# A 64-byte touch of every sixteenth QKV weight row, issued from ScalarE's queue ahead of the weight loads

## The chip, the cores and the metric

One core of a Trainium2 chip. The metric is device time in microseconds (us) of one execution; lower is better. Each execution also has a span, the time from its first to its last instruction, which is on record to 0.1 us. PE's granted clock is the share of its full clock that it was given, a mean over the execution. Engines: PE is TensorE (PEld its weight loads), DVE VectorE, ACT ScalarE, POOL GpSimd, SP SyncE; a "q" behind a name is its DMA-issuing queue.

## The reference, cut to what matters

```python
def reference(A_x, A_wqkv, A_wo, B_x, B_w_gate, B_w_up, B_w_down):
    x = A_x                                   # 1 x 2048 x 640, bf16
    xn = layernorm(x)
    # A: q, k, v = xn @ A_wqkv (640 x 1920); 32 heads of 20; each position attends
    #    to 8 earlier ones, 2 apart; then @ A_wo
    # B: ((xn @ w_gate) * (xn @ w_up)) @ w_down, 640 -> 1536 -> 640
    return x + A(xn) + B(xn)
```

Everything waits for the layer norm and for the first matmuls with `A_wqkv`, so the kernel begins with loads of x tiles (128 rows each) and of the QKV weights in chunks of 128 rows. The Q part, the K part and the V part of one weight row stand side by side in memory.

## The kernel before

The kernel records its operations with what each reads and writes, and derives the waits from that. The opening loads, in the order of issue:

```python
    op("act", ... ACT.Sqrt ..., name="sqrt_preload")
    for half, eng in ((0, "sp"), (1, "act")):          # x tile 0, half from each queue
        dst = XST[:, 0, half * DHALF:(half + 1) * DHALF]
        dma(dst, xhbm[0:TS, half * DHALF:(half + 1) * DHALF], w=[dst], name=f"xh{half}", eng=eng)
    x_load(1)                                          # all that follows is issued by SP
    for c in range(NCH):                               # NCH = 5
        wqkv_load(0, c)                                # Q weights, 160 KB a chunk
    x_load(2)
    x_load(3)
    for c in range(NCH):
        wqkv_load(1, c)                                # K weights
    ...
```

And the start of PE's work. Tile 0's Q projection goes through the chunks in order; of the five transposes of x tile 1, two stand between chunk 3 and chunk 4 and three within chunk 4:

```python
    bm = 1
    proj_tile(0, [(0, 0)], bm, {(4, 0): lambda: ln_pe(1, 0, 2), (4, 3): lambda: tr(1, 2)})
    part_evac(0, 0, 1, 0, 4, 0, 0)
    proj_tile(0, [(1, 2)], bm)
    ...
```

Of the kernel before, what the change touches and what calls it, by code (L numbers as in the profile page):

```python
# [10 lines left out]
D = 640  # L11
# [30 lines left out]
class Sched:  # L42
# [20 lines left out]
    def keys(self, x):  # L63
# [10 lines left out]
        for step, n in reversed(dims[1:]):  # L74
# [4 lines left out]
            else:  # L79
                starts = [s + i * step for s in starts for i in range(n)]  # L80
        if name == "PS":
            spans = {(s * es // 2048, (s + run - 1) * es // 2048) for s in starts}
# [130 lines left out]
def build_kernel(nc, A_x, A_wqkv, A_wo, B_x, B_w_gate, B_w_up, B_w_down, out):  # L213
# [5 lines left out]
    def sb(name, shape, dtype=BF16, at=None):  # L219
        n = mybir.dt.size(dtype)  # L220
        for s in shape[1:]:
            n *= s
        n = (n + 63) // 64 * 64
        if at is None:
            at = place[0]
            place[0] += n
        assert at + n <= 229344, (name, at + n)
        return K.sbuf(name, shape, dtype, at)
# [9 lines left out]
    a_pv = place[0]  # L238
# [46 lines left out]
    IDENT = sb("IDENT", [128, 128])  # L285
    MASK = sb("MASK", [128, W, PAD], FP16)
    MSK0 = sb("MSK0", [128, W, PAD], FP16)
    PS = nc.alloc_psum_tensor("PS", [128, 8, 512], FP32)
    xhbm = A_x[0]
    ohbm = out[0]  # L290

    def dma(o, i, r=(), w=(), name="", eng="sp", group=None):
        return op(eng, lambda e: e.dma_start(o, i), r=r, w=w, dma=True, name=name, group=group)
# [10 lines left out]
    op("dve", lambda e: e.memset(MASK[:], 0.0), w=[MASK[:]], name="mask0")  # L304
    op("dve", lambda e: e.memset(MSK0[:], 0.0), w=[MSK0[:]], name="msk0")
    op("pool", lambda e: e.affine_select(MSK0[:], MSK0[:], pattern=[[DIL, W], [1, PAD]], compare_op=ALU.is_ge, fill=NEG,
                                         base=-PAD, channel_multiplier=0), r=[MSK0[:]], w=[MSK0[:]], name="msk1")

    def x_load(t, eng="sp"):
        dma(XST[:, t % NXS, :], xhbm[t * TS:(t + 1) * TS, :], w=[XST[:, t % NXS, :]], name=f"xld{t}", eng=eng)  # L310
# [7 lines left out]
    def wqkv_load(g, c=None, eng="sp"):  # L318
        cs = slice(0, NCH) if c is None else c
        dst = WQKV[:, g, cs]  # L320
        dma(dst, wqkv_src[:, cs, g * D:(g + 1) * D], w=[dst], name=f"ld_wqkv{g}_{c}", eng=eng)

    op("act", lambda e: e.activation(DUM[:, 0:1], EPSC[:, 0:1], ACT.Sqrt), r=[EPSC[:]], w=[DUM[:]], name="sqrt_preload")
    for half, eng in ((0, "sp"), (1, "act")):
        dst = XST[:, 0, half * DHALF:(half + 1) * DHALF]
        dma(dst, xhbm[0:TS, half * DHALF:(half + 1) * DHALF], w=[dst], name=f"xh{half}", eng=eng)
    x_load(1)
    for c in range(NCH):
        wqkv_load(0, c)
# [12 lines left out]
    def late_loads():  # L342
        dma(MASK[0:128:4], MSK0[0:32], r=[MSK0[0:32]], w=[MASK[0:128:4]], name="mask")
        wqkv_load(2)
        for T, src in ((WG, B_w_gate), (WU, B_w_up)):
            dma(T[:], src.rearrange("(c p) n -> p c n", p=128), w=[T[:]], name="ld_w")
# [10 lines left out]
    def tp_view(t, c0, c1):  # L357
# [3 lines left out]
        if t == 1 and c0 > 1:  # L361
            b = 4
        return PS[:, b, :].bitcast(BF16)[:, c0 * 128:c1 * 128].rearrange("p (c f) -> p c f", c=c1 - c0)

# [82 lines left out]
    def warm(n, wide=JB):  # L447
        z = ZERO[:, 0:1].to_broadcast([128, wide])
        for _ in range(n):
            op("pe", lambda e: e.matmul(PS[:, 5, 0:wide], ZERO[:], z, start=True, stop=True), r=[ZERO[:]], w=[PS[:, 5, :]],  # L450
               name="warm")
# [9 lines left out]
    def wcols(which, c, m):  # L461
        return WQKV[:, which, c, m:D:NCH]
# [5 lines left out]
    def proj(which, m, j):  # L468
        b = bank()
        for c in range(NCH):  # L470
            l, x = wcols(which, c, m), XNT[:, c, j * JB:(j + 1) * JB]
            op("pe", (lambda l, x, c: lambda e: e.matmul(PS[:, b, :], l, x, start=(c == 0), stop=(c == NCH - 1)))(l, x, c),  # L472
               r=[l, x], w=[PS[:, b, :]], name=f"p{which}_{m}_{j}_{c}")
        if which == 2:
            o = VO[:, m, VP + j * JB:VP + (j + 1) * JB]
        else:
            o = qk_dst(which, m, j * JB, JB)
        sc = SCALE if which == 0 else 1.0
        op("act", lambda e: e.activation(o, PS[:, b, :], ACT.Copy, scale=sc), r=[PS[:, b, :]], w=[o],
           name=f"pev{which}_{m}_{j}")  # L480
# [463 lines left out]
def bass_parallel_sum__sliding_local_dilated__glu_gated_bilinear__prompt_kernel(  # L944
    nc, A_x, A_wqkv, A_wo, B_x, B_w_gate, B_w_up, B_w_down, out
):
    build_kernel(nc, A_x, A_wqkv, A_wo, B_x, B_w_gate, B_w_up, B_w_down, out)
# [28 lines left out]
```

## Time and profile before

| | |
|---|---|
| time, median of the first 3 runs | 254.32 us (254.29 to 254.47) |
| span of the profiled run | 252.4 us |
| PE busy | 98% |
| PE's share of the chain that ended last | 96% |
| start of PE's unbroken run | 7.84 us |

How to read it: PE is the bound nearly everywhere. What isn't PE lies in the first 8 us, where x tiles and weights come in and the first layer norms run. The chain of waits before begins PE's first group without further stops, 57 matmuls, at 7.84 and ends with the last addition on DVE:

```profile
7.84 3.32 PE PS L500 x57
...
250.20 0.22 DVE FOUT L691
```

(Columns: start, duration in us, engine and what.) From the first of these to the second are 242.36 us. If the start moves and the distance stays, the end moves with the start.

### The profile page before, as it was taken

The numbers are of one execution on the slowest core, as the hardware profiler recorded it, in microseconds if no ns is written. First come the engines' busy times: TensorE is split into PE (matmuls) and PEld (weight loads), VectorE is DVE, ScalarE is ACT, GpSimd is POOL, SyncE is SP. The second block draws the span as 40 slices with busy tenths as digits, with TensorE's granted clock in tenths as the row PEclk, the third lists the DMA queues.
The fourth block names the chain that finished last, engine by engine and source line by source line (L and its number), as shares of the span: only waits on it lengthen the run. The fifth ranks groups of instructions, "written<-read, shape, count | busy, mean of one in ns | idle before, by whom it ended". The sixth has DMA issues, their size and how long they took to land.

```text
span 252.4 us, 3908 instructions
## 1 busy us (share of the span) xinstructions
PE 248.1 (98%) x1607; PEld 149.2 (59%) x1622; DVE 215.1 (85%) x254; ACT 113.9 (45%) x202; POOL 35.9 (14%) x44
## 2 busy tenths in 40 slices
PE   8999999999999999999999999999999999999996
PEld 3999855555544444444444457764444777777775
DVE  4899799999999954999999974899999999995221
ACT  5486675555555557555555552225555112112000
POOL 1000001044425331003411100101000010111000
DMA  6988789956777562536379931393000021330511
GB/s 201 297 177 164 117 205 395 277 109 114 134 137 128 92 125 44 199 134 124 57 138 314 429 101 23 37 347 55 0 0 0 3 32 20 55 45 9 104 52 52
DMA packets 25664, 31.83 MB, mean 126 GB/s; under 512 B 9744, under 2 KB 22160, under 8 KB 25616
## 3 DMA queue, kind: packets, MB, share of 16 engines
q1 hardware_dynamic: 19120, 22.15, 28.9%
q0 software_dynamic: 6240, 9.31, 23.0%
q8 instruction: 12, 0.20, 0.3%
q10 hardware_dynamic: 288, 0.15, 0.2%
q14 instruction: 4, 0.03, 0.0%
HBM read 14.42 MB, written 4.59 MB: 75 GB/s over the span
## 4 chain that ended last, share of the span: by engine, by line
PE 96%; ACT 1%; DMA 1%; DVE 1%; issue 0%
PE PS L646 41%; PE PS L677 29%; PE PS L472 17%; PE PS L487 4%; PE PS L507 2%; PE PS L500 2%; DMA XST<-in_A_x_dram 1%; ACT XNS L391 0%; PE PS L431 0%; ACT XNS L389 0%; DVE STATS L369 0%; DVE STATS L375 0%; DVE XNS L416 0%; ACT SD L394 0%; ACT SD L382 0%
## 5 line engine op out<-in xcount | busy, mean ns | idle before, releaser
L646 PE MATMUL PS<-XNT,WU 128*128 128x512 bf16 x240 | 59.6, 379 | 0.0
L646 PE MATMUL PS<-XNT,WG 128*128 128x512 bf16 x229 | 57.3, 379 | 0.6
L613 DVE TENSOR_TENSOR PVB<-VO,ATB 128x10240 f16<-128x10240 bf16 x8 | 43.9, 5492 | 0.1
L677 PE MATMUL PS<-WD,HT 128*128 128x320 bf16 (+2 forms) x300 | 43.2, 294 | 0.0
L472 PE MATMUL PS<-XNT,WQKV 128*128 128x512 bf16 x196 | 43.0, 379 | 0.2
L646 PEld LDWEIGHTS PS<-XNT,WU 128*128 128x128 bf16 x240 | 23.5, 98 | 28.3
L646 PEld LDWEIGHTS PS<-XNT,WG 128*128 128x128 bf16 x240 | 23.5, 98 | 28.1
L648 ACT ACTIVATE USX<-PS 128x512 bf16<-128x512 f32 x48 | 28.7, 597 | 22.2 <-PE PS L646 21.7
L677 PEld LDWEIGHTS PS<-WD,HT 128*128 128x128 bf16 x300 | 28.7, 98 | 11.0
L472 PEld LDWEIGHTS PS<-XNT,WQKV 128*128 128x128 bf16 x200 | 23.5, 118 | 19.5
L608 DVE TENSOR_TENSOR PVB<-PVB 128x5120 f16<-128x5120 f16 (+1 forms) x16 | 34.6, 2160 | 0.3
L541 POOL DMA_DIRECT2D LOG<-PE x24 | 21.9, 939 | 60.9 <-DMA LOG<-PE 60.9
L648 ACT ACTIVATE HT<-PS 128x512 bf16<-128x512 f32 x36 | 21.5, 597 | 16.8 <-PE PS L646 16.8
L686 ACT ACTIVATE FACC<-PS 128x640 f16<-128x640 f32 x12 | 8.4, 703 | 44.1 <-PE PS L677 44.1
L677 PE MATMUL PS<-WO,VO 128*128 128x320 bf16 (+2 forms) x165 | 27.1, 295 | 0.0
L677 PEld LDWEIGHTS PS<-WO,VO 128*128 128x128 bf16 x165 | 15.9, 98 | 5.9
L530 DVE TENSOR_TENSOR PP<-QH,KH 128x2048 f16<-128x2048 bf16 x16 | 19.1, 1221 | 0.0
L530 DVE TENSOR_TENSOR TMP<-QH,KH 128x2048 f16<-128x2048 bf16 x16 | 19.0, 1221 | 0.0
L535 DVE TENSOR_TENSOR PP<-PP,TMP 128x4096 f16<-128x4096 f16 x8 | 18.3, 2292 | 0.2
L701 POOL DMA_DIRECT2D out_dram<-FACC x6 | 7.1, 1186 | 74.7 <-ACT FACC L686 74.7
L541 POOL DMA_DIRECT2D PE<-PP x8 | 8.7, 1089 | 61.3 <-DVE PP L536 61.3
L691 DVE TENSOR_TENSOR FOUT<-PS,XR 128x320 bf16<-128x320 f32 (+2 forms) x9 | 4.1, 454 | 15.3 <-PE PS L677 15.2
(67 smaller groups left out, 229.7 us busy)
## 6 DMA issues: line engine op xcount, KB each, us to landing
PE<-PP POOLq DMA_DIRECT2D x8, 512.0 KB, 5.0
ATB<-LOG SPq DMA_DIRECT2D x8, 512.0 KB, 4.3
LOG<-PE POOLq DMA_DIRECT2D x24, 128.0 KB, 2.7
WG<-in_B_w_gate_dram SPq DMA_DIRECT2D x1, 1920.0 KB, 9.3
WU<-in_B_w_up_dram SPq DMA_DIRECT2D x1, 1920.0 KB, 17.3
WD<-in_B_w_down_dram SPq DMA_DIRECT2D x1, 1920.0 KB, 10.1
out_dram<-in_A_x_dram SPq DMA_DIRECT2D x1, 1920.0 KB, 11.0
out_dram<-FACC POOLq DMA_DIRECT2D x6, 320.0 KB, 4.6
```

The source lines that it names most:

```text
L472: op("pe", (lambda l, x, c: lambda e: e.matmul(PS[:, b, :], l, x, start=(c == 0), stop=(c == NCH - 1)))(l, x, c), r=[l, x], w=[PS[:, b, :] ...
L487: op("pe", (lambda o, l, x, st, sp: lambda e: e.matmul(o, l, x, start=st, stop=sp))(o, l, x, st, sp), r=[l, x], w=[o], name=f"pp{which}_{m ...
L530: return (1.22, lambda: op("dve", lambda e: e.tensor_tensor(o, qw, kw, ALU.mult), r=[q, k], w=[o], name=f"prod{h}_{p}_{c}"))
L535: (2.3, lambda: op("dve", lambda e: e.tensor_tensor(a, a, b, ALU.add), r=[a, b], w=[a], name=f"psum{h}_{p}")),
L541: op("pool", lambda e: e.dma_start(o, i, accum_op=ALU.add), r=[o, i], w=[o], dma=True, name=name)
L608: return lambda: op("dve", lambda e: e.tensor_tensor(o, x, y, ALU.add), r=[x, y], w=[o], name=f"{name}_{b}")
L613: lambda: op("dve", lambda e: e.tensor_tensor(PVB[:], vw, aw, ALU.mult), r=[v, a], w=[PVB[:]], name=f"pv_{b}")),
L646: op("pe", (lambda l, x, c: lambda e: e.matmul(PS[:, b, :], l, x, start=(c == 0), stop=(c == NCH - 1)))(l, x, c), r=[l, x], w=[PS[:, b, :] ...
L648: op("act", lambda e: e.activation(o, PS[:, b, :], ACT.Copy), r=[PS[:, b, :]], w=[o], name=f"guev{which}_{m}_{j}")
L677: op("pe", (lambda l, x, i, b, wid: lambda e: e.matmul(PS[:, b, 0:wid], l, x, start=(i == 0), stop=(i == n - 1)))(l, x, i, b, wid), r=[l, ...
L686: op("act", (lambda o, i: lambda e: e.activation(o, i, ACT.Copy))(o, i), r=[PS[:, b - 1, :], PS[:, b, :]], w=[o], name=f"fin{t}")
L701: stores.append(op("pool", lambda e: e.dma_start(d, f, accum_op=ALU.add), r=[f, ("out",)], w=[("out", t)], dma=True, name=f"oacc{t}"))
```

## The change

The intent: a first read of a stretch of memory might be slow, so a tiny DMA reads something of every 16 rows of the weights ahead of their loads (16 rows of 3840 bytes are some 60 KB). It goes out on ACT's queue, which has nothing else to issue then. What it reads is never used; it lands in a place that another buffer takes over later.

```diff
+    PRE = sb("PRE", [D // 16, 32], at=a_pv)
...
         dma(dst, xhbm[0:TS, half * DHALF:(half + 1) * DHALF], w=[dst], name=f"xh{half}", eng=eng)
+    dma(PRE[:], A_wqkv[0:D:16, 0:32], w=[PRE[:]], name="touch", eng="act")
     x_load(1)
```

I call this DMA the touch.

## The prediction

> **What bounds the kernel now.** I read the page first: the busy shares, then the chain that ended last, then the waits. The busy table says which engine can hold the end, the chain says whether it does.
>
> ```profile
> span 252.4 us, 3908 instructions
> PE 248.1 (98%) x1607; PEld 149.2 (59%) x1622; DVE 215.1 (85%) x254; ACT 113.9 (45%) x202; POOL 35.9 (14%) x44
> ...
> PE 96%; ACT 1%; DMA 1%; DVE 1%; issue 0%
> ```
>
> PE is busy 98% of the span and is 96% of the chain. The chain in order of time shows where the other 4% lie:
>
> ```profile
> 0.74 2.05 DMA XST<-in_A_x_dram
> ...
> 4.27 0.73 ACT XNS L389 x2
> ...
> 6.51 0.36 DVE XNS L416
> 6.86 0.08 issue
> 6.94 0.45 PE PS L500 x5
> 7.39 0.11 PE PS L431 x2
> ```
>
> (Columns: start, duration in us, what.) Until 6.94 us the chain is load of x tile 0, its layer norm, then that of tile 1. After 6.94 PE is on the chain almost alone up to 250.17 us. So the change can reach the end only through the first 7 us, or by opening a hole in PE later. It touches only loads of the first microseconds, so I look at these closely. The timeline of the weight loads on PE at 5 to 8 us:
>
> ```profile
> 5.62 0.95 PEld L500 LDWEIGHTS PS<-XNT,WQKV 128*128 128x128 bf16 x15
> 6.91 0.32 PEld L500 LDWEIGHTS PS<-XNT,WQKV 128*128 128x128 bf16 x5 [0.34 <-DVE XNS L416]
> 7.17 0.15 PEld L431 LDWEIGHTS PS<-IDENT,XNS 128*128 128x128 bf16 x2
> 7.30 0.21 PEld L500 LDWEIGHTS PS<-XNT,WQKV 128*128 128x128 bf16 x3
> ```
>
> The first 15 are the Q projection of tile 0 on weight chunks 0, 1 and 2 (five each), the next five are chunk 3. They stood idle 0.34 us. The profile names DVE's XNS, but in the program these five matmuls don't use that result: the first of them waits for the load of Q weight chunk 3 and for an old copy on DVE. The two transposes behind them are what needs XNS. So I set the time of the load against it. The DMA view, one issue at a time (the last number is us from the issue to landing), for Q weight chunks 0, 2 and 3, issued by SP at 1.67, 2.61 and 3.08:
>
> ```profile
> WQKV<-in_A_wqkv_dram SPq DMA_DIRECT2D x1, 160.0 KB, 2.8
> WQKV<-in_A_wqkv_dram SPq DMA_DIRECT2D x1, 160.0 KB, 3.1
> WQKV<-in_A_wqkv_dram SPq DMA_DIRECT2D x1, 160.0 KB, 3.7
> ```
>
> Chunk 3 lands at 3.08 + 3.7 = 6.8, and the weight load starts at 6.91. This is the true releaser. Chunk 4 (issued at 3.56, 3.7 to landing) lands at about 7.3, just where the three matmuls at 7.30 begin. So the QKV loads do lie on the path, but for some tenths of a microsecond only, and the layer norm of tile 1 (XNS done at 6.51 + 0.36 = 6.87) ends nearly at the same time.
>
> **What the Trainium skill says, and whether the trace agrees.**
> "DMA: Bandwidth & Descriptors", section "Why a DMA increments its semaphore by 16 and not by 1", has a DMA from this kind of queue split over the largest count up to 16 that divides the slowest dimension. The new DMA has 40 rows, so 10 of the 16 engines get it, 4 pieces each. No run has shown that yet.
> The same page, "Issuing engines are not separate DMA queues", says that DMAs from different issuers run on the same 16 engines and interleave. So the new pieces do compete with SP's loads. The trace agrees: between 2 and 4 us the queue of ACT (q10) and that of SP (q1) both have packets at a DMA share of 0.97.
> "Perfetto Trace Analysis", section "DMA Instruction — HWDGE (DVE, Sync)", says the descriptor generator is shared and locked while one sequencer uses it. The trace of before doesn't show a cost of it: ACT's issue (1.00 to 1.38) overlaps SP's second (1.20 to 1.62), and that one takes 0.42 us, like the later ones at 0.43.
> I found no section on a first access to HBM being slower than later ones; the change rests on that idea.
>
> **The change part by part.** It removes nothing. Compared engine by engine, the order of PE, POOL and SP is the same; ACT gains one DMA issue behind its half of x tile 0, DVE gains one wait.
>
> 1. ACT's issue. The issue before it took 0.38 us (1.00 to 1.38), so the new one stands at about 1.4 to 1.8. ACT's next work that waits is the square root of tile 0:
>
> ```profile
> 1.00 0.38 ACTq L293 DMA_DIRECT2D XST<-in_A_x_dram  x1
> 2.04 0.20 ACT L323 ACTIVATE DUM<-EPSC 128x1 f32<-128x1 f32 x1
> 3.98 0.29 ACT L382 ACTIVATE SD<-MV,EPSC 128x1 f32<-128x1 f32 x1 [1.74 <-DVE MV L381]
> ```
>
> ACT is free for 1.74 us before that. Cost on the path: 0.
>
> 2. DVE's wait. The destination lies where a product buffer is written first after 33.99 us; the new DMA will have landed by some 4 us. A wait that is already met costs DVE at most some tens of ns, and at that place PE doesn't wait for DVE. Cost: 0.
>
> 3. DMA time. ACT's queue had 144 packets of 640 bytes at 14.1% of 16 engines over 2 us, which is 4.5 us / 144 = 31 ns each. SP's had 483 packets at 83.3%, or 55 ns each, mostly 1280 bytes. A 64-byte piece should take no more than the 31 ns (estimate). Four on one engine are 0.12 us, on 10 engines of 16. They would start about 1 us after the issue, near 2.4 us: the issue of the first x half at 0.74 is followed by data only in the slice from 1.6 to 2.0 us. The first weight chunk, issued 1.67, would start at about 2.7. So the touch stands before it or between its packets. If an engine that carries the touch is also the last for chunk 3, that chunk slips by up to 0.12 us, and PE by that. x tile 1 lands at 1.20 + 2.2 = 3.4 and ACT takes it at 4.18, so 0.12 there is covered. Cost on the path: 0 to +0.12 us.
>
> 4. The gain that is meant. If the first read of each stretch of weights is slow, and the touch takes that ahead, the chunks land sooner. The most that PE can gain: the 0.34 us of idle weight loading before chunk 3, less what the layer norm of tile 1 still imposes. The transposes need XNS at 6.87, and start loading at 7.17. So with the weights there in time PE moves forward by at most 7.17 - 6.9 = 0.27 us, and only when chunk 4 comes earlier too. Gain on the path: 0 to -0.27 us.
>
> The lead of the touch on chunk 0 is short, about 2.7 - 2.4 = 0.3 us, and chunks 3 and 4 start a good deal later, so it could have helped those most. But a hint in the profile is against slow first reads: the K chunks are other columns of the same rows that the Q chunks have read, and their loads took 3.5, 4.1, 4.0, 4.0 and 3.9 us to land against 2.8, 2.8, 3.1, 3.7 and 3.7 for Q. The queue was then longer, so it is a hint only. The DMA share and rate are alike too: 0.84 at 266 GB/s in 4 to 6 us, 0.99 at 311 in 8 to 12.
>
> Sum: 254.32 + 0 + 0 + (0 to 0.12) - (0 to 0.27), with neither likely in full. I weigh both at about a third, +0.04 and -0.09, and stay at 254.3.
>
> **The rivals.**
> A. Warm-up works: chunks 3 and 4 land 0.3 us sooner, PE starts its long run 0.2 to 0.27 us sooner, 254.1. For it: PE did wait for chunk 3. Against it: the K loads were no faster on rows already read.
> B. The touch delays: the generator is busy for ACT, so SP's row of issues shifts by up to one issue, 0.4 us, or the scattered small reads are much slower than 31 ns. Chunks 3 and 4 land 0.1 to 0.4 us later and PE with them: 254.4 to 254.7. Against it: the overlap of ACT's and SP's issues at 1.2 us cost nothing.
> C. It is hidden: the landings stay within 0.1 us and the layer norm of tile 1 sets the start anyway: 254.3. It fits best with nearly equal times of both (6.8 for chunk 3, 6.87 for XNS).
> None leads to 2%: that would be 5.1 us, and the whole stretch before PE's long run is 6.9 us of which the QKV loads set 0.3.
>
> **Range and chances.** The three runs of before spread over 0.18 us. The mechanism adds -0.27 to +0.4. Together with some run-to-run spread I take 253.9 to 254.8. Over 2% either way would need something that no view here hints at, such as a lower granted clock; 1% each.
>
> **What would show it.** In the changed profile: one more ACT queue issue near 1.4 us, and ACT's square root still at about 3.98; ACT's DMA queue with some 50 packets more; SP's weight issues still at 1.67, 2.13, 2.61, 3.08 and 3.56 (later ones speak for B's lock); the weight loads of chunk 3 at 6.91 within 0.15 (earlier by 0.2 or more, with chunk 3's landing time below 3.5 us, is A; later is B). The end should shift by exactly what the start of the 57-matmul group at 7.84 shifts; if the end moves by more than that, a later stage has changed and my reading that only the first 7 us count is wrong. I am wrong as a whole if the time leaves 253.9 to 254.8, above all if a DVE or PE wait appears after 30 us.

## The result, and the profile after

| | before | changed |
|---|---|---|
| time, median of 6 runs | 254.34 us (254.14 to 255.10) | 254.34 us (254.18 to 255.21) |
| ratio | | 1.0002 (95%: 0.9983 to 1.0021) |
| span of the profiled run | 252.4 us | 252.5 us |

A ratio is the mean time of one kernel's runs over that of the other's of the same rounds, so it isn't quite the ratio of the medians in the table. The page of the changed kernel; the third line is ACT's DMA queue (packets, MB, share), the fourth the chain by engine:

```profile
span 252.5 us, 3925 instructions
PE 248.7 (98%) x1622; PEld 149.0 (59%) x1622; DVE 215.4 (85%) x254; ACT 114.0 (45%) x202; POOL 35.9 (14%) x44
...
q10 hardware_dynamic: 338, 0.15, 0.2%
...
PE 96%; DMA 2%; SPq 1%; issue 0%; DVE 0%
```

Before, that queue had 288 packets; the touch adds 50: 40 pieces and 10 completions. (PE's count of 1607 before against 1622 here is records missing from the trace of before, not work added.) The chain in order of time, for its start and its end:

```profile
3.08 3.81 DMA WQKV<-in_A_wqkv_dram
6.89 0.14 issue
7.03 0.45 PE PS L502 x5
...
7.93 3.31 PE PS L502 x57
...
250.28 0.22 DVE FOUT L693
```

(Lines are one or two higher than before, as the change adds two.) The chain now runs through the load of Q chunk 3, issued at 3.08 and landed 3.81 us later. PE's run starts 0.09 us later than in the first trace, and the end is 0.08 us later. The distance from one to the other is 242.35 us, the same as before. The timeline around it:

```profile
1.42 0.61 ACTq L294 DMA_DIRECT2D PRE<-in_A_wqkv_dram  x1
1.66 2.33 SPq L294 DMA_DIRECT2D WQKV<-in_A_wqkv_dram  x5
3.92 0.29 ACT L384 ACTIVATE SD<-MV,EPSC 128x1 f32<-128x1 f32 x1 [1.68 <-DVE MV L383]
7.03 0.45 PE L502 MATMUL PS<-XNT,WQKV 128*128 128x128 bf16 x5 [0.46 <-DMA WQKV<-in_A_wqkv_dram]
```

The touch is issued at 1.42, SP's weight issues stand where they were, and ACT's square root isn't held up. This time the profile itself names the weight load as what PE waited for, where in the trace of before it named DVE (for the weight loads of these matmuls it still names DVE). The DMA view, for Q chunks 0, 2 and 3 as in the prediction (the last number is us from issue to landing):

```profile
WQKV<-in_A_wqkv_dram SPq DMA_DIRECT2D x1, 160.0 KB, 3.3
WQKV<-in_A_wqkv_dram SPq DMA_DIRECT2D x1, 160.0 KB, 3.4
WQKV<-in_A_wqkv_dram SPq DMA_DIRECT2D x1, 160.0 KB, 3.8
```

They took 2.8, 3.1 and 3.7 before. x tile 1 took 2.8 us where it had taken 2.2. So in this pair of traces the touch, meant to make loads faster, stands beside slower ones, by 0.5 us for chunk 0 and by 0.1 for chunk 3, which is the one that counts. One pair of traces can't tell the touch from the spread between executions, so the experiments begin there.

### The profile page after: what moved, and what is told of

Its sections match the earlier page's. It is cut to its first block, busy times and chain, and to the rows that moved or that the text cites. A ratio compares the mean times of both kernels' runs of the same rounds, so it can differ in the third digit from the quotient of the medians.

```text
span 252.5 us, 3925 instructions
## 1 busy us (share of the span) xinstructions
PE 248.7 (98%) x1622; PEld 149.0 (59%) x1622; DVE 215.4 (85%) x254; ACT 114.0 (45%) x202; POOL 35.9 (14%) x44
## 4 chain that ended last, share of the span: by engine, by line
PE 96%; DMA 2%; SPq 1%; issue 0%; DVE 0%
PE PS L648 41%; PE PS L679 29%; PE PS L474 17%; PE PS L489 4%; PE PS L509 2%; PE PS L502 2%; DMA WQKV<-in_A_wqkv_dram 2%; SPq L294 1%; PE PS L433 0%; DVE FOUT L693 0%
## 5 line engine op out<-in xcount | busy, mean ns | idle before, releaser
L648 PE MATMUL PS<-XNT,WG 128*128 128x512 bf16 x240 | 59.6, 379 | 0.0
```

The source lines that it names most:

```text
L648: op("pe", (lambda l, x, c: lambda e: e.matmul(PS[:, b, :], l, x, start=(c == 0), stop=(c == NCH - 1)))(l, x, c), r=[l, x], w=[PS[:, b, :] ...
```

## The experiments

Four questions: is a difference of 0.1 us in one pair of traces anything at all; does the touch warm anything; what does the touch cost where it has to be paid; and how much could better loads be worth? Theory H: it is hidden, neither cost nor gain gets beyond the spread. Rival D: it really delays the first loads. Rival W: the read ahead warms something, and the gain is lost on its own cost or for want of lead.

### 1. Both kernels again (rep_before, rep_after)

No edit.

> The kernel before once more, for the spread of the landing times from one execution to the next. Theory H (hidden, the touch costs PE about nothing and its cost lies within the spread): Q weight chunk 0 lands anywhere from 2.7 to 3.4 us after its issue, x tile 1 from 2.1 to 2.9, the weight loads of chunk 3 start at 6.8 to 7.1. Rival D (the touch really delays the first loads by half a microsecond): x tile 1 again 2.1 to 2.3 and chunk 0 again 2.7 to 2.9, chunk 3's weight loads at 6.91 within 0.05. Time 254.3 in both.

> The changed kernel once more. H: landing times mix with those of the kernel before; chunk 3's weight loads start between 6.8 and 7.1. D: x tile 1 again 2.7 to 2.9 us to landing, chunk 0 3.2 to 3.4, chunk 3's weight loads at 7.0 within 0.05. Time 254.3 within 0.3 in both.

Measured: rep_before 254.15 us, ratio 0.9984 (0.9967 to 1.0001); rep_after 254.35 us, ratio 0.9991 (0.9975 to 1.0006). In the repeat of the kernel before, PE hardly stopped for chunk 3 (20 weight loads in a row, the first of chunk 3 at 6.78), and x tile 1 and chunk 0 took 2.3 and 2.8 us:

```profile
5.70 1.40 PEld L500 LDWEIGHTS PS<-XNT,WQKV 128*128 128x128 bf16 x20
7.04 0.15 PEld L431 LDWEIGHTS PS<-IDENT,XNS 128*128 128x128 bf16 x2
```

The chain of that trace names neither a load nor the layer norm: it is PE's own work from 0.99 us on. In the repeat of the changed kernel, PE stood before chunk 3 until 6.91 and then waited for chunk 4, which took 4.0 us and is on the chain:

```profile
6.91 0.33 PEld L502 LDWEIGHTS PS<-XNT,WQKV 128*128 128x128 bf16 x5 [0.35 <-DVE SD L403]
7.18 0.15 PEld L433 LDWEIGHTS PS<-IDENT,XNS 128*128 128x128 bf16 x2
7.59 0.21 PEld L502 LDWEIGHTS PS<-XNT,WQKV 128*128 128x128 bf16 x3 [0.27 <-DMA WQKV<-in_A_wqkv_dram]
```

The 57-matmul group started at 7.72 and 8.13 us in the two repeats and the end came at 250.13 and 250.46: distances of 242.41 and 242.33.

Of D's numbers, those of x tile 1 (2.3 and, with the touch, 2.7 us) came back; those of chunk 0 with the touch (3.0, not 3.2 to 3.4) and of PE's weight loads didn't. Which chunk stops PE, and for how long, changes from one execution to the next. The two traces without the touch start PE at 7.84 and 7.72, the two with it at 7.93 and 8.13. That looks like a cost of a quarter of a microsecond, but it is two against two. There are more spans than traces: every timed execution has one.

| kernel | executions | mean span | range |
|---|---|---|---|
| before, all rounds of these experiments and its repeat | 29 | 252.55 us | 252.3 to 253.1 |
| changed, result and repeat | 10 | 252.49 us | 252.3 to 252.7 |

The changed kernel is 0.06 us shorter on average, with a standard error of 0.06 (0.04 and 0.05 from the scatter of the two rows). The executions come from several calls (a call builds a few kernels and executes them in turn); in the three calls of these experiments the mean span of before is 252.55 to 252.61. So over all executions neither a cost nor a gain can be seen. At two standard errors a cost above 0.06 us is excluded, and a gain above 0.18; a smaller gain has to be sought in the landings. The +0.08 us of the first pair lies within the spread.

How could the four traces mislead? In each of them the span is 244.6 to 244.7 us longer than the start of the 57-matmul group. So mean spans of 252.55 and 252.49 stand for mean starts of about 7.95 and 7.89 (estimates). The two traces of before, at 7.84 and 7.72, happened to be early ones.

### 2. The same touch on rows that nobody needs yet (touch_gate)

```diff
-    dma(PRE[:], A_wqkv[0:D:16, 0:32], w=[PRE[:]], name="touch", eng="act")
+    dma(PRE[:], B_w_gate[0:D:16, 0:32], w=[PRE[:]], name="touch", eng="act")
```

> The same DMA from the same queue at the same place, but it reads every sixteenth row of the gate weights, which nobody loads before 34 us: all the cost of the touch, none of its warmth for QKV. If warmth is worth anything, Q chunks 0 to 4 land later here than in the changed kernel, by 0.2 us or more, and the long run of PE starts later by as much. H and D: the same landing times as the changed kernel within 0.2 us, time the same within 0.2.

Measured: 254.33 us, ratio 0.9990 (0.9971 to 1.0009); spans 252.1 to 252.6, mean 252.45. The five Q chunks took 2.9, 3.2, 4.0, 4.0 and 3.9 us to land. The two traces of the changed kernel have 3.3, 3.2, 3.4, 3.8, 3.8 and 3.0, 2.9, 3.0, 3.7, 4.0. So chunks 0, 1, 3 and 4 agree within 0.4 us and chunk 2 is 0.6 us or more later here. Of the last two, which are on the path, chunk 3 is 0.2 to 0.3 us later here, just what the warmth theory asked for, and chunk 4 is not. But the kernel before, with no rows touched, took 3.7 and 3.6 us for chunk 3, no more than the 3.8 and 3.7 with the right rows. And PE's 57-matmul group started at 8.06, between the 7.93 and 8.13 of the changed kernel, so the start isn't later by 0.2. Chunk 2 is left as a hint of warmth; experiment 4 tests it with a better design.

### 3. The touch from SP's queue, and a touch of every row (touch_sp, touch_640)

```diff
-    dma(PRE[:], A_wqkv[0:D:16, 0:32], w=[PRE[:]], name="touch", eng="act")
+    dma(PRE[:], A_wqkv[0:D:16, 0:32], w=[PRE[:]], name="touch", eng="sp")
```

> The touch issued from SP instead of ACT, so that x tile 1 and all weight loads are issued one issue later (some 0.45 us). If the landing of Q chunk 3 sets the start of PE's long run, as I read it, chunk 3's weight loads start at about 7.0 to 7.4 and the span grows by 0.1 to 0.45 us. If the layer norm of tile 1 sets it (x tile 1 had 0.7 us of slack), the start stays at 6.9 within 0.1. If the DMA engines rather than the issues bound the landings, the slip of chunk 3 is much smaller than 0.45.

Measured: 254.42 us, ratio 0.9999 (0.9981 to 1.0017); spans 252.5, 253.2, 252.5, 252.6. The weight issues began at 2.03 instead of 1.66, the weight loads of chunk 3 started at 7.02, and the 57-matmul group at 7.94. A shift of all weight issues by 0.37 us thus delayed PE by only 0.1 to 0.2 us against the two traces of before (7.84 and 7.72). Chunks 0 and 3 made up for part of it: they landed 2.5 and 3.5 us after issue, against 2.8 and 3.6 to 3.7, and so within 0.3 us of where they had landed. Chunks 1 and 2 did not: 3.4 and 3.5 us against 2.8 to 2.9 and 3.1 to 3.3, so they landed 0.6 to 1.0 us later, and PE stopped for each (its weight loads went on at 5.99 and 6.50). So a later issue isn't a landing later by the same amount; that a backlog on the DMA engines is the reason isn't shown. A start of 7.02 for chunk 3's weight loads stands at the edge between the first two branches of the expectation and doesn't decide between them.

```diff
-    PRE = sb("PRE", [D // 16, 32], at=a_pv)
+    PRE = sb("PRE", [128, NCH, 32], at=a_pv)
...
-    dma(PRE[:], A_wqkv[0:D:16, 0:32], w=[PRE[:]], name="touch", eng="act")
+    dma(PRE[:], A_wqkv.rearrange("(c p) n -> p c n", p=128)[:, :, 0:32], w=[PRE[:]], name="touch", eng="act")
```

> A 64-byte piece of every row: 640 pieces instead of 40, 40 on each of 16 engines. If a piece costs only its packet time (11 ns in the trace), the engines lose 0.44 us and x tile 1 and the first chunks land some 0.3 to 0.6 us later than before, PE's long run starts 0.2 to 0.5 us later: span 252.7 to 253.0. If four pieces cost 0.45 us (what x tile 1 lost in the changed kernel), 40 cost 4.5 us and the span grows to 255 or more. If warmth were worth much, it would be seen here as well, as loads later than chunk 0 that take less than in the kernel before.

Measured: 255.12 us in the median (254.07 to 255.33), ratio 1.0016 (0.9990 to 1.0043); spans 252.5, 252.3, 253.5, 253.5. In the profiled run, one of the quick ones, the 57-matmul group started at 7.87. ACT's DMA queue between 2 and 4 us (packets, MB, share of 16 engines):

```profile
q10 hardware_dynamic: 752, 0.12, 36.9%
```

The same window in a kernel without a touch, no_w34 of experiment 6:

```profile
q10 hardware_dynamic: 144, 0.08, 13.8%
```

The 608 packets more took 0.231 of 32 engine-microseconds, which is 7.4 us or 12 ns each. (The packed traces have each packet: the touch's 64-byte ones took 11 ns in the median in both traces of the changed kernel.) At that, forty pieces on one engine are about 0.5 us and the four of the real touch 0.05 us. x tile 1 took 3.0 us here, 0.2 to 0.3 more than with four pieces on ten engines, and PE's start didn't move beyond the spread. So "half a microsecond for four pieces", one reading of the first trace, falls: ten times the pieces on an engine would have cost some 5 us. But a touch of this size has used up a slack: the chain of touch_640 begins with x tile 1 (issued at 1.20, landed 3.02 us later, at 4.22) and goes on with ACT's sums on it at 4.25. That two of four executions here have a span of 253.5, at a clock of 1.0, isn't explained; no trace of those two exists. With them the mean span is 252.95 against 252.61 for the kernel before in the same call, so a cost of this larger touch is not excluded.

What of x tile 1? It took 2.2 and 2.3 us in the two traces of before, and 2.7, 2.8 and 2.8 with the touch on ACT's queue. But it took 2.8 in no_w34, which has no touch, and only 2.2 to 2.5 in the four lead kernels below, which have the touch but hold the weights back. So a delay by the touch where touch and weights compete is possible, and not shown. In the changed kernel it doesn't reach PE: the tile has landed by 1.20 + 2.8 = 4.0, and ACT takes it behind tile 0's square root, which runs from 3.92 to 4.21.

### 4. A touch with all the lead it needs (lead_qkv, lead_gate, each twice)

```diff
-        dma(dst, wqkv_src[:, cs, g * D:(g + 1) * D], w=[dst], name=f"ld_wqkv{g}_{c}", eng=eng)
+        dma(dst, wqkv_src[:, cs, g * D:(g + 1) * D], r=r, w=[dst], name=f"ld_wqkv{g}_{c}", eng=eng)
...
-        wqkv_load(0, c)
+        wqkv_load(0, c, r=[PRE[:]])
```

(With `r=()` added to the arguments of `wqkv_load`.) SP waits for the touch before it issues Q chunk 0. lead_gate has the edit of touch_gate on top.

> The touch of the QKV rows with all the lead it can have: SP issues Q chunk 0 only when the touch has landed, so the weight loads start some 2 us later on idle DMA engines. The kernel must be 1.5 to 3 us slower for the wait itself (about 256 to 257.3). Warmth theory: Q chunk 0 lands clearly sooner after its issue than in the gate version below, by 0.3 us or more. No-warmth theory: the same within 0.2 us.

> The same wait, but the touch reads the gate weights, so the QKV rows are as cold as in the kernel before. Warmth theory: slower than the QKV version by 0.3 us or more, Q chunk 0 later after its issue by as much. No-warmth theory: times and landings within 0.2 us of the QKV version.

> The kernel with the awaited touch of the QKV rows once more, with more rounds, because the first pair differed by 0.28 us in mean span (254.02 against 254.30), at the edge of what four runs can show. Warmth: mean span again 0.2 us or more below the gate version of this same call, Q chunk 2 landing some 2.8 us after its issue. No warmth: the two means within 0.15 us.

> The same wait with the gate rows touched. Warmth: mean span 254.2 to 254.4, chunk 2 landing 3.1 us after its issue as in the first look. No warmth: within 0.15 us of the QKV version, chunk 2 anywhere from 2.7 to 3.2.

Measured: 255.88 and 256.10 us in the first call, 256.74 and 256.16 in the second (QKV rows first). The touch lands 2.1 to 2.3 us after its issue, and Q chunk 0 then starts on idle DMA engines. Its landing after issue, and that of chunk 3, in the DMA view of lead_qkv (QKV rows touched):

```profile
WQKV<-in_A_wqkv_dram SPq DMA_DIRECT2D x1, 160.0 KB, 2.2
WQKV<-in_A_wqkv_dram SPq DMA_DIRECT2D x1, 160.0 KB, 3.2
```

The same two in lead_gate (gate rows touched):

```profile
WQKV<-in_A_wqkv_dram SPq DMA_DIRECT2D x1, 160.0 KB, 2.2
WQKV<-in_A_wqkv_dram SPq DMA_DIRECT2D x1, 160.0 KB, 3.3
```

Chunk 0, on rows freshly touched or not, takes 2.2 us in all four traces. The mean spans were 254.02 against 254.30 in the first call, 0.28 us in favour of warmth, and I took that for a possible effect. In the second call they were 254.75 against 254.30, the other way round. But there four of the twelve executions had a granted clock of 0.993, three with the QKV rows and one with the gate rows, and these four are the longest (255.1 to 255.7; the rest reach from 253.7 to 254.4). At full clock the second call has 254.17 (three executions) against 254.12 (five). Both calls together, at full clock, give 254.09 against 254.20, with a standard error of the difference of 0.11. That is within the 0.15 that the no-warmth theory allowed. The hint of chunk 2 fell too: it took 2.8 us against 3.1 (gate) in the first pair of traces, but 3.2 against 3.0 in the second.

### 5. As much warmth as there can be (full_qkv, full_gate)

```diff
-    PRE = sb("PRE", [D // 16, 32], at=a_pv)
+    PRE = sb("PRE", [128, NCH, D], at=a_pv)
...
-    dma(PRE[:], A_wqkv[0:D:16, 0:32], w=[PRE[:]], name="touch", eng="act")
+    dma(PRE[:], A_wqkv.rearrange("(c p) n -> p c n", p=128)[:, :, 0:D], w=[PRE[:]], name="touch", eng="act")
```

(With the wait of experiment 4; full_gate reads the same size from `B_w_gate`.)

> The most warmth that can be had: the very bytes of all five Q chunks (800 KB) are read into scratch first, SP waits for that, and then loads them again. Slower than before by some 4 to 5 us for the wait. Warmth: chunks 0 to 4 land 0.3 us or more sooner after their issue than in the gate version. No warmth: the same within 0.2 us, spans within 0.3.

> The same size read from the gate weights instead: same wait, cold QKV rows. Warmth: chunks 0 to 4 later by 0.3 us or more and the span longer by as much. No warmth: equal to the QKV version within 0.2 us per landing and 0.3 us of span (the wait itself may differ by some tenths, as the first reads take what they take).

Measured: 260.76 and 260.67 us, 6.4 us more than before and not the 4 to 5 that I had expected; SP issued Q chunk 0 at 7.73 and 7.93 instead of 1.66. Mean spans were 258.95 and 258.72, each from four executions that spread over 1 us or more. Their granted clock was 0.987 to 1.0; in both traces it was 0.987: PE had almost nothing to do from about 6 to 10 us, and its clock was 0.50 from 10 to 16 us in full_qkv and from 8 to 14 in full_gate. So here the landings are to be compared and not the spans. Q chunks 0 to 4 took 2.1, 2.4, 2.6, 3.3 and 3.6 us after the same bytes had been read, and 2.2, 2.3, 3.1, 3.1 and 3.1 after other bytes had been. Chunk 2 is sooner and chunks 3 and 4 are later with the bytes read before. The sum of the five is 14.0 against 13.8. A quicker second read should show in chunk 0 above all, which has no backlog before it, and that differs by 0.1. Rival W falls as far as these runs can resolve: reading the very same bytes ahead does nothing for the next read that they show. One thing stays untested: whether rows that an earlier execution has read still count as cold. If they don't, there was nothing left to warm in any of these kernels.

### 6. What the best loads could be worth (no_w34)

The kernel before, with a wrong result: tile 0's Q matmuls of chunks 3 and 4 take chunk 0's weights, so nothing waits for those two loads there. The loads still run.

```diff
-                l, x = wcols(which, c, m), XNT[:, c, t * TS:(t + 1) * TS]
+                l, x = wcols(which, 0 if which == 0 and t == 0 and c >= 3 else c, m), XNT[:, c, t * TS:(t + 1) * TS]
```

> The kernel before, with a wrong result on purpose: tile 0's Q matmuls of chunks 3 and 4 use chunk 0's weights, so they need not wait for those two loads (the loads still run). It gives what the best possible warm-up of chunks 3 and 4 could be worth. My step 4: PE's long run starts up to 0.27 us earlier and the span is 0.1 to 0.3 us shorter, 252.1 to 252.3. If the layer norm of tile 1 sets the start alone: 0 to 0.05.

Measured: 254.25 us, ratio 0.9995 (0.9976 to 1.0013). The weight loads on PE, and then a wait at 29 us:

```profile
5.35 1.26 PEld L500 LDWEIGHTS PS<-XNT,WQKV 128*128 128x128 bf16 x20
6.78 0.11 PEld L431 LDWEIGHTS PS<-IDENT,XNS 128*128 128x128 bf16 x2 [0.17 <-DVE XNS L416]
...
29.09 1.02 PEld L472 LDWEIGHTS PS<-XNT,WQKV 128*128 128x128 bf16 x6 [0.23 <-DMA XNT<-XNS]
```

The start of PE's run and the end, in the chain:

```profile
7.42 3.31 PE PS L500 x57
...
250.03 0.23 DVE FOUT L691
```

The transposes load at 6.78 instead of 7.17, and the 57-matmul group starts at 7.42 instead of 7.84. Not all of these 0.42 us are the loads' doing: tile 1's layer norm was earlier in this execution too (its XNS began at 6.38 on DVE, against 6.51 and 6.50 in the two traces of before), which leaves about 0.29 (an estimate); against rep_before, which started at 7.72, it is 0.30. And the end comes at 250.03 instead of 250.20 (rep_before: 250.13). Of the 0.42 us, 0.17 reach the end. Part goes in the next 5 us (PE's next group, of 200 matmuls, starts at 12.51 instead of 12.83, only 0.32 earlier), the rest at 29.09, where PE waits 0.23 us for a DMA transpose of a later x tile. The mean of four spans is 252.38, against 252.55 for the 29 of before, a difference of 0.17 with a standard error of 0.06. So a perfect warm-up of chunks 3 and 4, the only ones of the five that PE waited for in the traces of the two kernels, would have been worth about 0.2 us, or 0.1%.

No experiment points to a version that beats both kernels by more than the spread.

## Why the prediction was right or wrong, point by point

**The number.** Right, but it proves little: all that was forecast lay between -0.27 and +0.4 us, and the single executions of before already spread from 254.14 to 255.10 us. The two terms that were weighed in, +0.04 and -0.09, nearly cancel, and neither was seen. So the point-by-point account counts for more.

**The bound.** Right. PE is 96% of the chain in both kernels, and in four traces (two of each kernel) the distance from PE's unbroken run to the end is 242.33 to 242.41 us while the start moves by 0.41 us. The end follows the start.

**The true releaser of chunk 3's matmuls.** Right: I read the load where the profile named DVE; the changed kernel's profile names the load for the matmuls (0.46 us on PE, where before had 0.21), and with the wait for the load taken out (no_w34) the transposes behind come 0.39 us earlier. What I had not seen is that this wait is a matter of the execution. The weight loads stood idle for 0.34 us in the first trace of before, for 0.58 in the changed kernel's, and for hardly any time in rep_before.

**Step 1, ACT's issue, cost 0.** Right in its effect: the square root began at 3.92 against 3.98. The size was off: the issue took 0.61 us, not 0.4. ACT's slack of 1.74 us covered it.

**Step 2, DVE's wait, cost 0.** Right. Where DVE first writes the buffer over the touch's landing place it goes on without a gap:

```profile
31.33 2.35 DVE L532 TENSOR_TENSOR PP<-QH,KH 128x2048 f16<-128x2048 bf16 x2
33.60 2.35 DVE L532 TENSOR_TENSOR TMP<-QH,KH 128x2048 f16<-128x2048 bf16 x2
```

**Step 3, DMA time, 0 to +0.12 us.** The ten engines with four pieces each fit the 50 packets, 40 pieces and 10 completions; the split that the Trainium skill gives for 40 rows ("DMA: Bandwidth & Descriptors", section "Why a DMA increments its semaphore by 16 and not by 1") agrees with them. The bound of 31 ns a piece was more than twice too large: touch_640 gives 12 ns, so 0.05 us per engine. (The 144 packets that I divided by were not all of 640 bytes: 16 of them are completions.) Nothing of it shows in 10 spans against 29.

**Step 4, the gain, 0 to -0.27 us.** In the sum I gave it a third of its size, -0.09 us. This term should have been nought: the lead and full kernels show no warmth that they could resolve. The reason I gave against it, K loads that were no quicker on rows already read, pointed the right way. The ceiling of 0.27 was about right for PE's start (0.29 to 0.30 in no_w34, once its earlier layer norm is taken off). As a ceiling for the end it was too high, for I took it that the start carries over in full: 0.17 got there.

**The rivals.** A (warm-up works) fails by its own signs: chunk 3 took 3.8 and 3.7 us in the two traces of the changed kernel against 3.7 and 3.6 before, and PE's run started no sooner; experiments 4 and 5 find no warmth either. B's lock didn't hold SP up: its weight issues stand at 1.66 and after, as before, and the slow small reads of B are ruled out by the 12 ns. C (hidden) is what the spans show, but its picture holds only in part. Its landings should have stayed within 0.1 us, and chunk 0's moved by 0.2 to 0.5. And the layer norm of tile 1 doesn't set the start by itself: in the two traces of the changed kernel the chain runs through the loads of chunk 3 and of chunk 4, in rep_before through PE's own work. What is right is that several things end nearly together: with the loads taken out (no_w34) PE still waits 0.17 us for XNS before the transposes.

**Where my reading was incomplete.** I wrote that the change reaches the end only through the first 7 us. For a delay that stood up. For a gain it doesn't: no_w34 shows a second floor at 29 us, the transposes of later x tiles: PE's group there starts at 29.35 instead of 29.51, only 0.16 earlier.

**What stays open.** Why single executions at the full clock are 0.7 to 1.2 us longer than the shortest of their fellows (253.1 before, 253.2 with the touch from SP, 253.5 with 640 pieces). Only one execution per run left a trace here, and it wasn't one of those. The longest of the lead kernels (255.1 to 255.7) are those with the clock at 0.993; of them there is no trace either, so why the clock fell is open. And whether the weights' rows were cold in the first place, as said in experiment 5.

## What to carry to other kernels

Before a prefetch or warm-up is added, take the wait it is meant to shorten away altogether, even with a wrong result: that gives the most it can be worth, here 0.2 us of 254. Test warmth with a twin that reads other addresses at the same time and size, since a touch can delay things whatever it reads, and look at the granted clock of each execution before two means are compared. And with loads that end within tenths of a microsecond of each other, let the spans of many executions decide and not one pair of traces: here two traces of each kernel suggested a cost of 0.25 us that 39 spans don't show.

## What the Trainium skill lacked or had wrong

- "DMA: Bandwidth & Descriptors" says nothing on whether an earlier read makes a later read of the same HBM rows quicker, and I found no page that does. Here no such gain shows: chunk 0 landed 2.2 us after issue with its rows touched or not, and 2.1 against 2.2 after a full read of the same or of other bytes.
- "Perfetto Trace Analysis", section "DMA Instruction — HWDGE (DVE, Sync)", has the sequencer perform excess semaphore increments at the end of an issue, without a duration. Here the 40-row DMA, which fits 10 engines, took 0.61 us to issue from ACT, whether SP went on issuing beside it from 1.66 us on (the changed kernel) or stopped at 1.62 (lead_qkv), and 0.39 from SP; a 128-row one from ACT took 0.45 (touch_640). That the increments are the cause is not shown.
